# Chunk 3's normalized x through transposing transfers, eps as a column of x, PSUM banks by name, and a newly written order

## The chip, the cores and the metric

The kernel runs on one core of a Trainium2 chip. The metric is the device time of one execution in microseconds (us). The core has five engines with an instruction stream each: TensorE (PE, with its weight loads as PEld), VectorE (DVE), ScalarE (ACT), GpSimd (POOL) and SyncE (SP), which here issues transfers only. 16 DMA engines move the data.

## The reference

A linear-attention layer with a decay of its own for every channel, then a gated feed-forward block. B, H, S, D = 4, 8, 768, 48; the model width is H*D = 384, the feed-forward width 1536.

```python
for t in range(S):
    cur = einsum('bhd,bhe->bhde', u * k[t], v[t])
    y[t] = einsum('bhd,bhde->bhe', r[t], state + cur)
    state = w[t][..., None] * state + einsum('bhd,bhe->bhde', k[t], v[t])
x = y as (B*S, H*D)
rms = sqrt(mean(x * x) + 1e-06)
xn = x / rms * rms_g
g = xn @ w_gate
out = (g * sigmoid(g) * (xn @ w_val)) @ w_out
```

All inputs and the output are float32; the matmuls take bf16.

## The kernel before

The sequence is cut into chunks of 128 tokens, and a step is named `function.n.j`: n is the chunk (0 to 5), j mostly the batch (0 to 3) or, in the feed-forward part, a unit of work. Chunks 0 and 1 are the even and the odd tokens of the first 256, loaded together (384 KB per input and batch); later chunks are loaded one by one (192 KB).

Attention of one block (n, j): `ln` takes log w, `cs_mm`, `cs_k` and `cs_add` sum it over the tokens into PSUM, `exp_r` and `exp_k` exponentiate on ACT, `r_mul` (DVE) and `k_mul` (mostly POOL) multiply r and k into the tile `rk`. `rk` is transposed by PE (`rk_pe`, chunks 0 and 1) or by a transposing transfer (`rk_tr`, the others), `q_mm` makes the scores, `q_mask_e`, `q_copy_o` and `q_mask_o` mask them, `y_mm` makes y, `st_mm` and `st_new` carry the state. The bonus with u is `bonus_mul` (two products on POOL, tile `ruk`), `bonus_sum` (DVE, `diag`) and `bonus_v` (POOL, `ydiag`); `x_add` adds it to y.

Normalization of one block: `x_sq` sums the squares of 384 elements on ACT, `x_rstd` takes the reciprocal root (on ACT by Ln and Exp, or on POOL by a scaling and a power), `xn_mul` multiplies. For the feed-forward part, x must lie transposed in `xnt`. In chunks 0 to 3 `xn_pe` does this with three PE transposes into PSUM, and `xn_out` multiplies by rms_g on DVE on the way out. In chunks 4 and 5 `xn_tr` is a transposing transfer on SP's queue, and `xn_gain` multiplies by rms_g on POOL in place.

Feed-forward of one chunk: 12 units `gate_mm`, `silu` (ACT), `val_mm`, `h_mul` (DVE), then four `o_mm` (12 matmuls each, the last one of the last chunk in three pieces), `o_out`, `out_dma`. From chunk 1 on, a unit needs all four blocks of x of its chunk; in chunk 0 it needs two. The weights are cast on the way in by transfers that POOL issues: `load_gv.g.h` (gate h = 0, value h = 1; g = 1 is the larger part, feature blocks 4 to 11) and `load_wo`. All other transfers stand in SP's queue.

The order is a written list, `ORDER`: its 1096 steps are emitted one after the other, and each engine runs its own instructions in that order, waiting on semaphores for the others. Nothing is scheduled beyond that. `warm` steps are matmuls on zeros (13 at the start, 21 in between).

The eight PSUM banks form three rings: "a" has two banks, "b" two, "q" four. Each function names its ring, and `psum` takes the bank of that ring whose last use lies farthest back in the list. In the profile a bank reads as `ps_au`, `ps_bv`, `ps_qx` and so on. Sets such as `XN_DVE` or `CAST_ACT` say block by block on which engine a step runs.

Of the kernel before, what the change touches and what calls it, by code (L numbers as in the profile page):

```python
# [10 lines left out]
FP32 = mybir.dt.float32  # L11
# [16 lines left out]
warm.210.0 warm.211.0 warm.212.0 load_w.0.0 load_w.0.1 ln.0.0 ln.0.1 load_r.0.0 load_k.0.0 cs_k.0.0 exp_k.1.0  # L28
k_mul.1.0 cs_mm.0.0 exp_k.0.0 gu_mm.0.0 load_r.0.1 gu_out.0.0 load_k.0.1 exp_r.0.0 k_mul.0.0 bonus_mul.0.0 exp_r.1.0
cs_mm.0.1 cs_k.0.1 exp_r.0.1 load_w.0.2 exp_k.0.1 r_mul.0.0 r_mul.1.0 load_w.0.3 r_mul.0.1 bonus_mul.0.1 bonus_mul.1.0  # L30
exp_k.1.1 load_k.0.2 rk_pe.0.0 rk_tr.0.0 k_mul.1.1 rk_pe.1.0 warm.13.2 warm.14.2 warm.15.2 load_v.0.0 k_mul.0.1
rk_tr.1.0 bonus_sum.0.0 w_tot.0.0 load_gv.1.0 exp_r.1.1 load_r.0.2 q_mm.0.0 warm.16.0 q_mm.1.4 warm.17.1 warm.18.2
q_mask_e.0.0 r_mul.1.1 ln.0.2 ln.0.3 q_copy_o.0.0 cs_k.0.2 q_copy_o.1.4 exp_k.1.2 cs_mm.0.2 w_tot.0.1 q_mask_e.1.4
bonus_v.0.0 load_v.0.1 q_mask_o.1.4 exp_k.0.2 q_mm.1.0 rk_pe.1.1 warm.19.1 warm.20.1 warm.21.2 q_copy_o.1.0
bonus_sum.0.1 q_mask_e.1.0 exp_r.0.2 k_mul.1.2 cast_v.0.0 q_mm.0.4 warm.22.0 load_r.0.3 bonus_sum.1.0 load_k.0.3
exp_r.1.2 q_copy_o.0.4 cast_v.1.0 rk_pe.0.1 rk_tr.0.1 q_mask_o.1.0 cs_mm.0.3 q_mask_e.0.4 rk_tr.1.1 r_mul.1.2
bonus_v.1.0 exp_k.0.3 exp_r.0.3 y_mm.0.0 warm.23.0 q_mm.0.5 warm.24.0 warm.25.2 x_add.0.0 q_copy_o.0.5 y_mm.1.0
q_mask_o.0.5 cast_v.1.1 q_mask_e.0.5 cast_v.0.1 load_v.0.2 r_mul.0.2 x_sq.0.0 x_add.1.0 rk_pe.1.2 load_w.2.0
load_w.2.1 rk_tr.1.2 q_mm.0.1 warm.26.0 warm.27.0 warm.28.0 warm.29.2 q_copy_o.0.1 q_mask_e.0.1 exp_r.1.3 load_gv.1.1
q_mm.1.1 warm.30.2 x_rstd.0.0 st_mm.0.0 k_mul.0.2 w_tot.0.2 x_sq.1.0 q_mask_e.1.1 xn_mul.0.0 load_v.0.3 bonus_v.0.1  # L40
x_rstd.1.0 y_mm.0.1 rk_pe.0.2 q_copy_o.1.1 load_w.2.3 w_tot.0.3 xn_pe.0.0 st_new.0.0 xn_mul.1.0 x_add.0.1 cs_k.0.3
rk_tr.0.2 exp_k.1.3 xn_out.0.0 x_sq.0.1 bonus_mul.1.1 r_mul.0.3 xn_pe.1.0 warm.31.1 warm.32.2 xn_out.1.0 q_mm.1.5
warm.33.1 gate_mm.0.2 silu.0.2 gate_mm.0.3 silu.0.3 q_mask_o.1.1 q_mask_e.1.5 x_rstd.0.1 bonus_sum.1.1 q_copy_o.1.5
q_mm.1.2 r_mul.1.3 load_r.2.0 k_mul.1.3 bonus_v.1.1 bonus_mul.0.3 y_mm.1.1 xn_mul.0.1 x_add.1.1 gate_mm.0.5
gate_mm.0.4 q_mm.1.6 q_mask_e.1.2 load_gv.0.0 k_mul.0.3 q_copy_o.1.2 q_mask_e.1.6 silu.0.5 load_gv.0.1 bonus_mul.1.2
rk_pe.1.3 rk_tr.1.3 val_mm.0.3 xn_pe.0.1 xn_out.0.1 h_mul.0.3 q_copy_o.1.6 x_sq.1.1 val_mm.0.5 x_rstd.1.1 q_mm.1.7
xn_mul.1.1 rk_pe.0.3 bonus_mul.0.2 load_wo.0.0 val_mm.0.2 load_w.2.2 h_mul.0.5 q_copy_o.1.7 xn_pe.1.1 xn_out.1.1
st_mm.0.1 val_mm.0.4 load_r.2.1 gate_mm.0.10 h_mul.0.2 val_mm.0.10 ln.2.0 cast_v.1.2 ln.2.1 st_new.0.1 bonus_sum.1.2
q_mask_e.1.7 silu.0.4 q_mm.0.2 silu.0.10 rk_tr.0.3 load_v.2.1 gate_mm.0.9 gate_mm.0.8 q_copy_o.0.2 cast_v.0.2 silu.0.9
# [84 lines left out]
def kernel(  # L134
# [610 lines left out]
```

## Time and profile before

| | us |
|---|---|
| median of 3 runs | 200.35 (199.78, 203.26, 200.35) |
| span of the profiled execution, first to last instruction | 197.6 |
| PE busy in it | 191.5 (97%) |
| DVE, ACT, POOL busy | 156.4, 139.1, 127.5 |
| first feed-forward unit on PE starts | 25.79 |

Of the profiled execution the span is known, not its time by the runs' clock; the median of the runs lies 2.75 us above the span. "Busy" is the time in which an engine had at least one instruction in work. PE's matmuls overlap, each lasting some 0.16 us longer than its distance to the next, so a busy PE may still hold short gaps.

### The profile page before, as it was taken

The page shows a single profiled execution, that of the slowest core. Times are in us where ns is not written, and L with a number is a line of the kernel's source. Part 1 is how long each engine was busy: PE and PEld are TensorE (multiplying, and loading weights), DVE is VectorE, ACT ScalarE, POOL GpSimd, SP SyncE. Part 2 cuts the span into 40 slices and gives each one's busy share as a digit, 9 for nine tenths or more (in the row PEclk, how much of TensorE's full clock was granted, in tenths as well). Part 3 has the DMA queues.
Part 4 walks back from the last instruction along what each step waited for, and adds up shares of the span by engine and source line. Part 5 has one row for each costly group of instructions (what it writes and reads, how often), then busy time and mean ns, then how long its engine had stood idle before and what let it go on. Part 6 is the DMA issues. An engine that isn't in the chain of part 4 may idle for free.

```text
span 197.6 us, 4751 instructions
## 1 busy us (share of the span) xinstructions
PE 191.5 (97%) x1742; PEld 120.4 (61%) x1742; DVE 156.4 (79%) x315; ACT 139.1 (70%) x286; POOL 127.5 (64%) x181
## 2 busy tenths in 40 slices
PE   7899999999999999999999999999999999999994
PEld 3456677888665556655655655666655655555563
DVE  5699998999997999989799988997689842435530
ACT  3989998979997889795699875698556760514201
POOL 3399999988599759793969998599661544000000
PEclk9999999999999999999999999999999999999999
DMA  6999999999897999999999967924580021012112
GB/s 164 320 325 267 244 220 205 220 213 197 174 230 162 199 179 214 200 211 214 185 206 225 202 147 166 227 51 145 134 216 12 5 60 60 20 63 80 40 60 101
DMA packets 109807, 32.42 MB, mean 164 GB/s; under 512 B 104276, under 2 KB 108632, under 8 KB 109784
## 3 DMA queue, kind: packets, MB, share of 16 engines
q1 hardware_dynamic: 107744, 28.58, 63.4%
q0 software_dynamic: 2032, 3.54, 10.0%
q8 instruction: 13, 0.21, 0.5%
q14 instruction: 10, 0.08, 0.1%
q10 hardware_dynamic: 8, 0.00, 0.0%
HBM read 25.96 MB, written 4.72 MB: 155 GB/s over the span
## 4 chain that ended last, share of the span: by engine, by line
PE 83%; DMA 7%; POOL 6%; SPq 1%; issue 1%; ACT 0%; POOLq 0%
PE ps_bu L646 13%; PE ps_bv L646 12%; PE ps_av L646 11%; PE ps_au L646 11%; PE ps_qv L683 7%; PE ps_qx L683 6%; PE ps_qz L683 6%; DMA wv_sb<-in_moe_w_val_dram 5%; PE ps_qu L683 5%; DMA kt<-in_k_dram 2%; POOL ruk L464 1%; POOL ruk L465 1%; SPq L248 1%; POOL qts L536 1%; PE ps_qz L513 1%
## 5 line engine op out<-in xcount | busy, mean ns | idle before, releaser
L238 ACT ACTIVATE sg<-ps_av 128x512 bf16<-128x512 f32 x36 | 21.5, 596 | 27.1 <-PE ps_av L646 21.4
L683 PEld LDWEIGHTS <-ht 128*128 128x128 bf16 x312 | 28.6, 98 | 18.3 <-DVE ht L666 0.4
L646 PEld LDWEIGHTS <-wg_sb 128*128 128x128 bf16 x252 | 27.0, 114 | 16.6 <-issue 0.3
L646 PEld LDWEIGHTS <-wv_sb 128*128 128x128 bf16 x252 | 26.4, 114 | 16.0 <-DMA wv_sb<-in_moe_w_val_dram 0.7
L666 DVE TENSOR_TENSOR ht<-ps_bu,sg 128x512 bf16<-128x512 f32 x37 | 25.4, 687 | 10.7 <-PE ps_bu L646 8.3
L666 DVE TENSOR_TENSOR ht<-ps_bv,sg 128x512 bf16<-128x512 f32 x35 | 24.0, 686 | 9.9 <-PE ps_bv L646 8.5
L646 PE MATMUL ps_bu<-xnt,wv_sb 128*128 128x512 bf16 (+1 forms) x135 | 30.3, 343 | 0.5 <-DMA wv_sb<-in_moe_w_val_dram 0.5
L646 PE MATMUL ps_av<-xnt,wg_sb 128*128 128x512 bf16 (+1 forms) x126 | 29.4, 350 | 0.0
L646 PE MATMUL ps_au<-xnt,wg_sb 128*128 128x512 bf16 (+1 forms) x126 | 29.3, 349 | 0.1
L646 PE MATMUL ps_bv<-xnt,wv_sb 128*128 128x512 bf16 (+1 forms) x117 | 28.5, 358 | 0.0
L464 POOL TENSOR_TENSOR ruk<-rt,kt 128x384 f32<-128x384 f32 x24 | 24.0, 1002 | 1.9 <-DVE diag L469 1.4
L465 POOL TENSOR_TENSOR ruk<-ruk,u_bc 128x384 f32<-128x384 f32 x24 | 24.0, 1000 | 1.9
L238 ACT ACTIVATE sg<-ps_au 128x512 bf16<-128x512 f32 x36 | 21.5, 596 | 4.5 <-PE ps_au L646 3.3
L457 POOL TENSOR_TENSOR rk<-kt,ek 128x384 bf16<-128x384 f32 x20 | 19.8, 1001 | 6.6 <-DMA kt<-in_k_dram 5.5
L475 POOL TENSOR_TENSOR ydiag<-vt,diag 128x384 f32<-128x384 f32 x24 | 19.9, 836 | 1.0 <-DVE diag L469 1.0
L236 ACT ACT_TABLE_LOAD x14 | 18.0, 1283 | 1.9 <-PEq L729 1.6
L536 POOL TENSOR_SCALAR_AFFINE_SELECT qts<-qts 128x512 bf16<-128x512 bf16 x19 | 11.9, 637 | 11.2 <-ACT qts L533 8.0
L683 PE MATMUL ps_qv<-wo_sb,ht 128*128 128x384 bf16 (+1 forms) x96 | 15.5, 311 | 0.0
L581 ACT ACTIVATE junk<-xb 128x384 bf16<-128x384 f32 x24 | 12.5, 521 | 4.2 <-DVE xb L576 3.9
L469 DVE TENSOR_REDUCE diag<-ruk 128x8 f32<-128x384 f32 x24 | 13.0, 544 | 0.0
L683 PE MATMUL ps_qx<-wo_sb,ht 128*128 128x384 bf16 x72 | 12.7, 326 | 0.0
L683 PE MATMUL ps_qz<-wo_sb,ht 128*128 128x384 bf16 x72 | 12.7, 326 | 0.0
(212 smaller groups left out, 376.8 us busy)
## 6 DMA issues: line engine op xcount, KB each, us to landing
out_dram<-ob SPq DMA_DIRECT2D x19, 192.0 KB, 2.4
wt<-in_w_dram SPq DMA_DIRECT2D x16, 192.0 KB, 4.2
rt<-in_r_dram SPq DMA_DIRECT2D x16, 192.0 KB, 4.4
vt<-in_v_dram SPq DMA_DIRECT2D x16, 192.0 KB, 3.7
kt<-in_k_dram SPq DMA_DIRECT2D x16, 192.0 KB, 4.0
wt<-in_w_dram SPq DMA_DIRECT2D x4, 384.0 KB, 4.3
rt<-in_r_dram SPq DMA_DIRECT2D x4, 384.0 KB, 4.9
kt<-in_k_dram SPq DMA_DIRECT2D x4, 384.0 KB, 4.9
```

What stands on the lines that cost most here:

```text
L236: nc.scalar.preload_act_table_set(table_name)
L238: return nc.scalar.activation(**kw).ins
L457: eng.tensor_tensor(out=rk[:, n % 2, j, 1, :, 0:D], in0=inp["k", n, j], in1=bank["cs_k", n, j][:, 0:DM].rearrange("p (h d) -> p h d", h=H) ...
L464: eng.tensor_tensor(out=ruk[n, j], in0=inp["r", n, j], in1=inp["k", n, j], op=ALU.mult)
L465: eng.tensor_tensor(out=ruk[n, j], in0=ruk[n, j], in1=u_bc, op=ALU.mult)
L469: nc.vector.tensor_reduce(out=diag[n, j].rearrange("p h o -> p (h o)"), in_=ruk[n, j], axis=mybir.AxisListType.X, op=ALU.add)
L475: eng.tensor_tensor(out=ydiag[n, j], in0=inp["v", n, j], in1=diag[n, j].to_broadcast([128, H, D]), op=ALU.mult)
L536: nc.gpsimd.affine_select(out=qts[n, j][:, 1], in_=qts[n, j][:, 1], compare_op=ALU.is_ge if n < 2 and j // 4 < n else ALU.is_gt, fill=0.0, ...
L581: nc.scalar.activation(out=junk, in_=xb[n, j], func=AF.Square, accum_out=rstd[n, j][:, 0:1])
L646: nc.tensor.matmul(ps.rearrange("p (i t) -> p i t", t=cols.stop - cols.start)[:, i, :], lhsT=units(ws, c, fs.start + i), rhs=xnt[n][:, c, ...
L666: nc.vector.tensor_tensor(out=ht[n][:, fs, cols], in0=bank.pop(("v", n, f)).rearrange("p (i t) -> p i t", i=fs.stop - fs.start), in1=bank. ...
L683: nc.tensor.matmul(ps[:, cols], lhsT=ht[n][:, f, b * L:(b + 1) * L], rhs=wo_sb[:, f, cols], start=(f == 0), stop=(f == FC - 1))
```

## The change

Chunk 3 joins chunks 4 and 5: its four blocks are transposed by `xn_tr` and multiplied by `xn_gain` on POOL. x gets a 385th column that holds sqrt(eps * 384), so that the sum of squares, now scaled by 1/384 inside `x_sq`, includes eps; the reciprocal root on POOL is then one instruction, not two. Three lists name steps whose PSUM bank comes from another ring than their function's. The order is written anew in all its 1090 steps (17 fillers in between instead of 21), and so are the sets that choose engines: 15 value casts on ACT instead of 13, 11 products by the root on DVE instead of 6, two of the first transposes copied out on DVE instead of four, 17 separate masks on POOL instead of 19, seven roots on ACT instead of eight. ACT has 12 table loads instead of 14.

```diff
-warm.210.0 warm.211.0 warm.212.0 load_w.0.0 load_w.0.1 ln.0.0 ln.0.1 load_r.0.0 load_k.0.0 cs_k.0.0 exp_k.1.0
+warm.210.0 warm.211.0 warm.212.0 load_w.0.0 ln.0.0 cs_mm.0.0 exp_r.0.0 w_tot.0.0 exp_k.0.0 load_r.0.0 exp_r.1.0
...
+    MOVED_Q = "cs_k.2.3 cs_k.3.1 ..."
+    MOVED_A = "cs_k.2.1 cs_k.3.0 ..."
+    MOVED_B = "cs_k.1.1 cs_r.0.0 ..."
...
+    moved = {}
+    for c, names in (("q", MOVED_Q), ("a", MOVED_A), ("b", MOVED_B)):
+        for x in names.split():
+            name, n, j = x.split(".")
+            moved[name, int(n), int(j)] = c
 
     def psum(ring, key, shape, dtype=FP32):
+        ring = moved.get(key, ring)
         slots = rings[ring]
...
+    xrow = const.tile([128, NXB, DM + 16], FP32)
+    nc.vector.memset(xrow[:, :, DM:DM + 1], (eps * DM) ** 0.5)
...
     def x_add(n, j):
-        xb[n, j] = pt.tile([128, DM], FP32, name="xb", bufs=NXB)
-        nc.vector.tensor_tensor(out=xb[n, j], in0=bank.pop(("y", n, j)),
+        k = min((x for x in range(NXB) if xslots[x][0] < at[0]), key=lambda x: xslots[x])
+        xslots[k] = [xlast[n, j], NXB + at[0]]
+        xb[n, j] = xrow[:, k, 0:DM + 1]
+        nc.vector.tensor_tensor(out=xb[n, j][:, 0:DM], in0=bank.pop(("y", n, j)),
...
     def x_sq(n, j):
-        nc.scalar.activation(out=junk, in_=xb[n, j], func=AF.Square, accum_out=rstd[n, j][:, 0:1])
+        nc.scalar.activation(out=junk[:, 0:DM + 1], in_=xb[n, j], func=AF.Square, scale=DM ** -0.5,
+                             accum_out=rstd[n, j][:, 0:1])
...
     def x_rstd(n, j):
-            act(LN_EXP, out=ss, in_=ss, func=AF.Ln, scale=1.0 / DM, bias=eps_col)
+            act(LN_EXP, out=ss, in_=ss, func=AF.Ln)
...
-            nc.gpsimd.tensor_scalar(out=ss, in0=ss, scalar1=1.0 / DM, scalar2=eps, op0=ALU.mult, op1=ALU.add)
             nc.gpsimd.tensor_tensor(out=rstd[n, j][:, 1:2], in0=ss, in1=mhalf, op=ALU.pow)
```

SP's queue at the very start, where the loads of the first 256 tokens stand (`wt`, `rt`, `kt` are w, r, k of a batch; the first of each is batch 0). Before:

```order
L248 DMA wt_167<-in_w_dram 128x8x96
L248 DMA wt_169<-in_w_dram 128x8x96
L248 DMA rt_174<-in_r_dram 128x8x96
L248 DMA kt_176<-in_k_dram 128x8x96
L248 DMA rt_203<-in_r_dram 128x8x96
L248 DMA kt_207<-in_k_dram 128x8x96
```

Now:

```order
L257 DMA wt_167<-in_w_dram 128x8x96
L257 DMA rt_190<-in_r_dram 128x8x96
L257 DMA kt_194<-in_k_dram 128x8x96
L257 DMA wt_208<-in_w_dram 128x8x96
L257 DMA wt_252<-in_w_dram 128x8x96
L257 DMA vt_294<-in_v_dram 128x8x96
```

r and k of batch 0 have moved ahead of w of batch 1, and k of batch 1 behind v of batch 0.

POOL's queue up to the larger part of the value weights (`wv_sb4`). Five rows are the same in both orders and stand ahead of these: one `k_mul` and two `bonus_mul`, of two rows each. Before:

```order
L464 TENSOR_TENSOR ruk_245<-rt_174,kt_176 128x384
L465 TENSOR_TENSOR ruk_245<-ruk_245,u_bc_76 128x384
L457 TENSOR_TENSOR rk_131<-kt_207,ek_235 128x8x48
L350 DMA wg_sb4_138<-in_moe_w_gate_dram 128x3x1024
L475 TENSOR_TENSOR ydiag_346<-vt_278,diag_283 128x384
L536 AFFINE_SELECT qts_314<-qts_314 128x512
L536 AFFINE_SELECT qts_363<-qts_363 128x512
L475 TENSOR_TENSOR ydiag_440<-vt_278,diag_402 128x384
L536 AFFINE_SELECT qts_474<-qts_474 128x512
L384 CAST vb_500<-vt_348 128x384
L350 DMA wv_sb4_140<-in_moe_w_val_dram 128x3x1024
```

Now:

```order
L471 TENSOR_TENSOR rk_129<-kt_315,ek_270 128x8x48
L550 AFFINE_SELECT qts_266<-qts_266 128x512
L489 TENSOR_TENSOR ydiag_406<-vt_294,diag_311 128x384
L478 TENSOR_TENSOR ruk_414<-rt_317,kt_315 128x384
L479 TENSOR_TENSOR ruk_414<-ruk_414,u_bc_76 128x384
L357 DMA wg_sb4_136<-in_moe_w_gate_dram 128x3x1024
L550 AFFINE_SELECT qts_289<-qts_289 128x512
L489 TENSOR_TENSOR ydiag_479<-vt_294,diag_275 128x384
L471 TENSOR_TENSOR rk_129<-kt_482,ek_376 128x8x48
L478 TENSOR_TENSOR ruk_524<-rt_317,kt_315 128x384
L479 TENSOR_TENSOR ruk_524<-ruk_524,u_bc_76 128x384
L357 DMA wv_sb4_138<-in_moe_w_val_dram 128x3x1024
```

The value weights now have one bonus pair (`ruk`, two rows) and one `k_mul` (`rk`) more ahead of them, and one mask and one cast fewer.

SP's queue where chunk 3 is normalized, now (before, no transposing transfer of `xn` stood there); the two transfers of batches 0 and 3 stand just ahead, `rt_2012` is r of chunk 4, batch 0:

```order
L622 DMA_TRANSPOSE xnt_2157<-xn_2211 128x3x128
L719 DMA out_0_dram<-ob_1938 128x384
L267 DMA rt_2012<-in_r_dram 128x8x48
L267 DMA vt_2221<-in_v_dram 128x8x48
L719 DMA out_0_dram<-ob_1845 128x384
L622 DMA_TRANSPOSE xnt_2157<-xn_2246 128x3x128
```

And POOL's queue there, now; the first row is the root of batch 2, `ruk_2298` the bonus of chunk 4, batch 0:

```order
L606 TENSOR_TENSOR rstd_2162<-rstd_2162,mhalf_126 128x1
L640 TENSOR_TENSOR xnt_2157<-xnt_2157,gT_77 128x3x128
L478 TENSOR_TENSOR ruk_2265<-rt_1553,kt_1926 128x384
L479 TENSOR_TENSOR ruk_2265<-ruk_2265,u_bc_76 128x384
L640 TENSOR_TENSOR xnt_2157<-xnt_2157,gT_77 128x3x128 x2
L478 TENSOR_TENSOR ruk_2298<-rt_2012,kt_1661 128x384
L479 TENSOR_TENSOR ruk_2298<-ruk_2298,u_bc_76 128x384
L640 TENSOR_TENSOR xnt_2157<-xnt_2157,gT_77 128x3x128
```

The four multiplications by rms_g stood on DVE before, and the last of them now follows the bonus of the next chunk.

More of the change, by code (lines that the diff above doesn't have):

```diff
@@ L325 @@
     nc.vector.memset(mhalf, -0.5)
-    eps_col = small.tile([128, 1], FP32)
-    nc.vector.memset(eps_col, eps)
     lw = persist.tile([128, 2, SB, H, PD], BF16)
@@ L360 @@
     bank = {}
+    xrow = const.tile([128, NXB, DM + 16], FP32)
+    nc.vector.memset(xrow[:, :, DM:DM + 1], (eps * DM) ** 0.5)
+    xlast = {(int(b), int(c)): i for i, (a, b, c) in enumerate(x.split(".") for x in ORDER.split())
+             if a in ("x_sq", "xn_mul")}
+    xslots = [[-2, i] for i in range(NXB)]
     def pair(t, q):
@@ L382, in cast_v @@
             nc.scalar.copy(out=vb[n, j], in_=inp["v", n, j])
+        elif (n, j) in CAST_DVE:
+            nc.vector.tensor_copy(out=vb[n, j], in_=inp["v", n, j])
         else:
```

233 lines of the change are left out of this document (116 added, 117 removed).

## The prediction

> **What bounds the kernel now.** I read the page from the top: the engines' shares and the granted clock, then the busy time in four stretches, then what TensorE (PE) waited for, then its instructions in order of time at the places that the change touches.
>
> ```profile
> span 197.6 us, 4751 instructions
> PE 191.5 (97%) x1742; PEld 120.4 (61%) x1742; DVE 156.4 (79%) x315; ACT 139.1 (70%) x286; POOL 127.5 (64%) x181
> PEclk9999999999999999999999999999999999999999
> ...
> 0.00:25.80 25.80, 23.15 (x269) 13.87 (x270) 21.95 (x61) 21.13 (x43) 19.09 (x33) 1.00 1.05 265
> 25.80:45.00 19.20, 18.71 (x254) 16.42 (x255) 18.21 (x33) 17.05 (x33) 17.73 (x25) 1.00 1.12 210
> 45.00:160.00 115.00, 114.98 (x1012) 70.03 (x1011) 103.18 (x202) 90.95 (x194) 86.96 (x120) 1.00 0.79 167
> 160.00:197.60 37.60, 34.70 (x212) 20.12 (x209) 13.09 (x22) 10.02 (x19) 3.67 (x6) 1.00 0.19 61
> ```
>
> The last four rows are stretches: length, then busy us and instructions of PE, PE's weight loads, DVE, ACT and POOL, the clock, the DMA share. From 45 to 160 us PE is busy for 114.98 of 115 us, and after that until its end: there PE is the bound, and only PE work that goes away, or a new wait of PE, moves the time. The other engines have slack there, though DVE little (103 of 115 us). The front is different. Busy PE flatters it: the matmuls overlap, and part of them are fillers on zeros.
>
> ```profile
> 4.22 0.53 PE L377 MATMUL ps_qx<-zero 128*128 128x384 bf16 x1
> 4.54 0.53 PE L377 MATMUL ps_qz<-zero 128*128 128x384 bf16 x1
> ...
> 21.59 0.32 PE L377 MATMUL ps_qz<-zero 128*128 128x384 bf16 x1
> 21.75 0.32 PE L377 MATMUL ps_bu<-zero 128*128 128x384 bf16 x1
> ...
> 25.79 0.82 PE L646 MATMUL ps_au<-xnt,wg_sb 128*128 128x256 bf16 x6
> 26.44 0.82 PE L646 MATMUL ps_av<-xnt,wg_sb 128*128 128x256 bf16 x6
> ```
>
> Columns are start, duration, instruction. The start-to-start distance is what a matmul takes from PE: a filler 0.32 us at first and 0.16 us later, a unit of six feed-forward matmuls 0.65 us (26.44 - 25.79). The first unit starts at 25.79 us. The front is fed by DVE, POOL and the weights' transfers:
>
> ```profile
> 8.13 0.56 DVE L457 TENSOR_TENSOR rk<-kt,ps_qv 128x384 bf16<-128x384 f32 x1 [1.67 <-DMA kt<-in_k_dram]
> ...
> 25.09 0.55 DVE L619 TENSOR_TENSOR xnt<-ps_qx,gT 128x384 bf16<-128x384 bf16 x1
> ...
> 1.92 1.26 SPq L248
> 3.23 4.80 DMA kt<-in_k_dram
> 20.98 9.76 DMA wv_sb<-in_moe_w_val_dram
> ...
> 30.79 0.84 PE L646 MATMUL ps_bu<-xnt,wv_sb 128*128 128x256 bf16 x6 [0.49 <-DMA wv_sb<-in_moe_w_val_dram]
> ```
>
> DVE starts its first product when k lands (3.23 + 4.80 = 8.03 us) and works without a gap to the second block of normalized x at 25.64. POOL issues the larger value-weight transfer at 20.98; it takes 9.76 us, and PE waits 0.49 us for it. That is one of only four waits of PE in the whole list, the first and the last of which are
>
> ```profile
> PE ps_qu L377 <- DVE half_of L303: 1.0, 1, 1.0
> ...
> PE ps_qv L377 <- DVE rkT L489: 0.3, 1, 0.3
> ```
>
> **The change part by part.**
>
> *Transposes of chunk 3.* Twelve PE transposes (four blocks of three) and four DVE multiplications go.
>
> ```profile
> 104.85 0.33 PE L612 MATMUL ps_qz<-ident,xn 128*128 128x128 bf16 x3
> 105.02 0.33 PE L612 MATMUL ps_qx<-ident,xn 128*128 128x128 bf16 x3
> 105.19 0.33 PE L410 MATMUL ps_au<-lw,mask_lt 128*128 128x384 bf16 x1
> ...
> xnt<-xn SPq DMA_TRANSPOSE x8, 2.3
> rt<-in_r_dram SPq DMA_DIRECT2D x16, 192.0 KB, 4.4
> ...
> 136.45 1.95 PE ps_qz L683 x12
> ```
>
> Three transposes take 0.17 us from PE (105.02 - 104.85), four blocks **0.7 us**, all in the stretch where PE is the bound: it comes off whole. The DVE multiplications are 4 x 0.55 = 2.2 us and hidden. What takes their place: four transposing transfers on SP's queue, 2.3 us each to land, and four multiplications on POOL. Chunks 4 and 5 go that way already, and no wait of PE is listed there. What is queued behind them matters more. On SP the transfer of batch 1 has r of chunk 4, batch 0, two places behind it; on POOL the bonus of that r stands ahead of the last multiplication of chunk 3, for which the first gate unit of chunk 3 waits. The chain from the reciprocal root of batch 1: its product with x (0.55 as the DVE row above), a transposing transfer (2.3 at most, since only its issue holds up the next), r (4.4 to landing), the bonus (2.0), the multiplication (0.84), together 10.1 us. PE has in the meantime three units of 0.65, three output products of 1.95 each and 0.7 us of small matmuls, 8.5 us. So a stall of up to 1.6 us is possible; but the root may run ahead of PE, whose own work on that stretch is not tied to it. Below nothing is excluded here: no PE work goes beyond the transposes. I take 0, nearest to chunks 4 and 5, and keep +1.6.
>
> *The front.* SP now loads w, r, k of batch 0 first, before w of batch 1; k is third instead of fourth, so up to 1.3 us sooner (one issue, 1.26 us). DVE has 38 instructions from its first product to the second block of normalized x in both orders; the new one has one wide instruction in place of one of the smallest, at most 0.6 us more. So the first gate unit would come between 0.7 us sooner and, if DVE is left waiting early on (its first sum over the bonus still needs three POOL products), 0.6 us later. But the value weights bind first. POOL's rows:
>
> ```profile
> L464 POOL TENSOR_TENSOR ruk<-rt,kt 128x384 f32<-128x384 f32 x24 | 24.0, 1002 | 1.9 <-DVE diag L469 1.4 <-DMA kt<-in_k_dram 0.5
> L465 POOL TENSOR_TENSOR ruk<-ruk,u_bc 128x384 f32<-128x384 f32 x24 | 24.0, 1000 | 1.9
> L475 POOL TENSOR_TENSOR ydiag<-vt,diag 128x384 f32<-128x384 f32 x24 | 19.9, 836 | 1.0 <-DVE diag L469 1.0
> L457 POOL TENSOR_TENSOR rk<-kt,ek 128x384 bf16<-128x384 f32 x20 | 19.8, 1001 | 6.6 <-DMA kt<-in_k_dram 5.5 <-ACT ek L238 1.0
> L536 POOL TENSOR_SCALAR_AFFINE_SELECT qts<-qts 128x512 bf16<-128x512 bf16 x19 | 11.9, 637 | 11.2 <-ACT qts L533 8.0 <-DMA vt<-in_v_dram 3.2
> L590 POOL TENSOR_TENSOR rstd<-rstd,mhalf 128x1 f32<-128x1 f32 x16 | 8.9, 556 | 1.3
> L625 POOL TENSOR_TENSOR xnt<-xnt,gT 128x384 bf16<-128x384 bf16 x8 | 6.6, 844 | 4.3 <-DMA xnt<-xn 3.4 <-PE ps_bu L646 1.0
> L589 POOL TENSOR_SCALAR rstd<-rstd 128x1 f32<-128x1 f32 x16 | 3.0, 189 | 8.9 <-ACT junk L581 8.2
> ...
> wv_sb<-in_moe_w_val_dram POOLq DMA_DIRECT2D x1, 384.0 KB, 7.5
> ...
> 42.16 0.85 PE L646 MATMUL ps_bu<-xnt,wv_sb 128*128 128x256 bf16 x6
> ```
>
> Ahead of the larger value-weight transfer POOL took 20.98 - 8.03 = 12.95 us after k. The new order puts one bonus pair (2.0) and one k product (1.0) more ahead of it and one select and one cast (0.64 each, the cast taken at the select's row) fewer: +1.7, so 14.7 us. With k at 6.8 to 8.0 us it is issued at 21.5 to 22.7 and lands 9.76 us later, at 31.3 to 32.4, which is 0.5 to 1.7 us after the 30.74 of now. Against that, PE has more done by then: one more group of eight transposes and two more score products of eight, at 0.057 us for a transpose (0.17 / 3) 0.45 us and 0.45 to 0.9 us, in all 0.9 to 1.35 us. The balance lies between 0.5 - 1.35 = -0.85 and 1.7 - 0.9 = +0.8; below that, up to the 1.3 us of k may come on top if DVE and not the weights bind. I take the early k, since the transfer order says it outright, and the smaller work: 0.5 - 0.9 = **-0.4 us**. The four fillers fewer (0.16 us each) are worth nothing by themselves: where a filler stood, PE waited for DVE.
>
> *Roots, casts, copies, eps, banks.* POOL loses the 0.19 us of scaling in each of its roots, two selects and two casts, and gains four multiplications (3.4 us); ACT loses two of 14 table loads; single casts and copies move between ACT, POOL and DVE. All of it lies under a full PE after 45 us and costs nothing there. The cover is thinnest on DVE: it gains five products of at most 0.55 us and loses 2.2 us, so about +0.5 us on 103 of 115; without cover, that 0.5 us would be the price. Drawing PSUM banks from any ring takes nothing from an engine. It can only remove waits of PE, of which the long stretch shows none.
>
> *The end.*
>
> ```profile
> 194.03 0.67 PE L683 MATMUL ps_qu<-wo_sb,ht 128*128 128x96 bf16 x12
> ...
> 194.74 0.24 ACT L692 COPY ob<-ps_qu 128x96 f32<-128x96 f32 x1 [0.54 <-PE ps_qu L683]
> ...
> L236 ACT ACT_TABLE_LOAD x14 | 18.0, 1283 | 1.9 <-PEq L729 1.6
> ```
>
> The last output piece is now 192 columns wide, not 96. PE's sum is unchanged; the copy after it grows from 0.24 us, at most to double: +0.1 us taken.
>
> *Sum*: span 197.6 - 0.7 - 0.4 + 0.1 = 196.6 us. The profiled execution's time is known as its span only; the median of the three runs, 200.35, stands 2.75 us above it, and I add this: **199.3 us**.
>
> One rule speaks against the change. In the rows above the fillers go from 0.32 to 0.16 us apart after about 4 us of matmuls, and the granted clock stays at 9 or more in every slice. The Trainium skill, "TensorE: Matmul & The Clock Gate", Part 1, says that the array runs at half clock until it has been busy for a window of about 3.4 us, and falls back after an idle window as long. The trace agrees with its first half (a halving of the distance between 4.54 and 21.59 us); no row shows a fall back. By the rule, fewer fillers could cost clock; it enters as the fourth case below.
>
> **The rivals.**
>
> *The front gains more (197.6 us).* If the first unit follows DVE and the weights are not waited for, the early k gives 1.2 us and the work done ahead 0.9 us: 197.6 - 0.7 - 2.1 + 0.1 = 194.9, and 2.75. For it: DVE is gapless from 8.13 us on. Against it: POOL's longer queue ahead of the weights.
>
> *Weights late (201.7 us), slower than before.* POOL sets the front. Between the two value-weight issues the new order has one k product less, but three selects, one cast and two roots more, against one root with its scaling (-1.0 + 1.9 + 0.64 + 1.1 - 0.75): +1.9 us on the 10.8 us of now, so the second is issued at 34.2 us or later and lands 7.5 us after that, 41.7. PE uses it at 42.16 now. With k at 8.0 us it lands at 42.9, and each wait of POOL for a diagonal or a mask adds. Then both weights cost: +0.8 and some 1.2, so 197.6 - 0.7 + 2.0 + 0.1 = 199.0, and 2.75. It decides at a landing of the first weights after about 32.2 us, or of the second after 42. Against it: the second transfer would follow the first at a greater distance and may land sooner than in 7.5 us.
>
> *Nothing comes of it (200.4 us).* The transposes' 0.7 us come back as a wait of the first gate unit of chunk 3, the chain of 10.1 against 8.5 us above.
>
> *The clock falls back (201 us).* If PE idled long enough in the first 25 us, one stretch of 3.4 us would run with matmuls twice as far apart, as at 4.22 us: up to 1.7 us more, 199.3 + 1.7. The granted clock of before speaks against it.
>
> **How the numbers follow.** Forecast 50% (198.4 to 200.2), front gains more 22%, weights late 18%, nothing 7%, clock 3%. The front's case spreads down to 195.5, the late weights' up to 203. The range takes 196.0 to 202.0 us: it leaves a third of the front's case and a third of the late weights' out, some 14%. Two per cent, about what a measurement can tell from no change here, are 196.3 and 204.4 us: faster 8%, within 89%, slower 3%.
>
> **What would show it.** Right: no transposes on PE between chunk 2's last and chunk 4's units, four transposing transfers and four multiplications for chunk 3, the first gate unit at 25 to 26.5 us, the larger value weights landing between 31 and 32.5 us, and PE at 115 of 115 us from 45 us on. Wrong: a wait of PE at the first gate unit of chunk 3 for POOL; a wait for the value weights above 1.5 us; distances of 0.32 us after 10 us; or a first gate unit before 24 us, which would mean that the front was bound by the order and not by DVE's sum.

## The result and the profile after

The changed kernel takes 208.1 us in the median of four runs (206.43 to 209.85), the kernel before 200.06; the ratio is **1.039 (1.033 to 1.045)**: slower. The forecast was 199.3 us. Runs that took over 1.5% longer than the fastest of their kernel stay out of every ratio, but not out of the medians.

The page of the changed kernel, top to bottom: its span, the busy time of each engine, the busy share of the DMA engines in 40 slices, and the chain that ended last, by engine and by line.

```profile
span 205.5 us, 4679 instructions
PE 191.3 (93%) x1711; PEld 120.5 (59%) x1726; DVE 158.0 (77%) x315; ACT 136.1 (66%) x280; POOL 126.2 (61%) x166
DMA  6999999999998899999977998602494012220012
PE 48%; DMA 13%; DVE 12%; POOL 10%; ACT 6%; issue 5%; SPq 4%; ACTq 0%; POOLq 0%; DVEq 0%
```

PE's sum is nearly the old one, 191.3 us against 191.5, in a span 7.9 us longer: the time is PE waiting. PE now holds 48% of the chain (83% in the kernel before), and transfers, DVE and POOL 35%. The stretches show where (length, then busy us of PE, its weight loads, DVE, ACT, POOL, the clock, the DMA share, GB/s):

```profile
30.00:45.00 15.00, 13.95 (x179) 12.83 (x177) 13.09 (x23) 12.31 (x22) 13.66 (x19) 1.00 1.13 210
45.00:60.00 15.00, 14.37 (x158) 10.81 (x158) 14.74 (x33) 14.31 (x34) 10.33 (x13) 1.00 1.02 201
60.00:75.00 15.00, 13.96 (x121) 7.80 (x121) 12.78 (x24) 9.23 (x18) 12.06 (x16) 1.00 0.91 190
75.00:90.00 15.00, 13.61 (x128) 8.50 (x131) 14.18 (x32) 13.39 (x34) 12.45 (x15) 1.00 1.01 206
90.00:105.00 15.00, 14.05 (x127) 8.23 (x129) 11.96 (x22) 8.88 (x20) 6.79 (x10) 1.00 1.05 219
105.00:120.00 15.00, 12.55 (x83) 7.19 (x84) 12.50 (x26) 10.50 (x20) 12.33 (x16) 1.00 0.83 164
120.00:165.00 45.00, 44.73 (x366) 26.26 (x370) 34.47 (x63) 27.88 (x61) 30.34 (x39) 1.00 0.54 117
```

PE is idle for 75 - 68.54 = 6.5 us between 45 and 120 us, where it had been full, and for 0.3 us after that to 165. The waits of PE in the list are many and short: nine between 45 and 120 us, 5.8 us in all. But for the 1.1 us of a filler at the very start, its longest are

```profile
PE ps_bu L424 <- DVE ht L678: 1.6, 1, 1.6
PE ps_au L628 <- DVE xn L611: 1.5, 2, 1.2
PE ps_av L424 <- DVE st L566: 0.9, 1, 0.9
PE ps_av L515 <- ACT sg L247: 0.7, 1, 0.7
PE ps_av L658 <- POOL xnt L640: 0.5, 1, 0.5
```

The fourth, and 0.3 us of the second, lie before 45 us. The last is the wait that the prediction looked for, of chunk 3's first gate unit for POOL: 0.5 us. Three of the other four name an instruction that has nothing to do with the data of the waiting matmul, but is the last reader of its PSUM bank (feed-forward product, state and activation): in the first, `cs_mm` (L424) of chunk 4 waits at 106.45 us for DVE's feed-forward product, which reads `ps_bu` until then. Why DVE was late there, the chain in order of time tells:

```profile
97.36 4.79 DMA rt<-in_r_dram
...
102.22 1.01 POOL ruk L478
...
103.30 1.00 POOL ruk L479
...
104.31 0.45 POOL vb L398
104.75 1.03 POOL rstd L606 x2
...
105.81 0.70 DVE xn L611
...
106.88 0.54 DVE diag L483
107.41 1.21 DVE ht L678 x2
```

An r of chunk 4, issued at 97.36 us, lands at 102.15. POOL's bonus product waits for it, and behind it in POOL's queue stand the cast and two reciprocal roots of chunk 3; behind the roots' product stand DVE's feed-forward products; behind them PE. A late input of one chunk stops the feed-forward of another through three engines that work in written order.

### The profile page after: what moved, and what is told of

It reads as the page before. It is cut to its first block, busy times and chain, and to the rows that moved or that the text cites. A ratio compares the mean times of both kernels' runs of the same rounds, so it can differ in the third digit from the quotient of the medians.

```text
span 205.5 us, 4679 instructions
## 1 busy us (share of the span) xinstructions
PE 191.3 (93%) x1711; PEld 120.5 (59%) x1726; DVE 158.0 (77%) x315; ACT 136.1 (66%) x280; POOL 126.2 (61%) x166
## 4 chain that ended last, share of the span: by engine, by line
PE 48%; DMA 13%; DVE 12%; POOL 10%; ACT 6%; issue 5%; SPq 4%; ACTq 0%; POOLq 0%; DVEq 0%
DMA wt<-in_w_dram 6%; PE ps_bv L658 4%; DMA kt<-in_k_dram 4%; PE ps_av L658 3%; SPq L267 3%; PE ps_bu L658 3%; PE ps_au L658 3%; PE ps_qu L658 3%; PE ps_qv L658 3%; PE ps_bv L695 3%; PE ps_au L695 3%; PE ps_qz L658 3%; POOL rk L471 2%; POOL ruk L478 2%; DMA rt<-in_r_dram 2%
## 5 line engine op out<-in xcount | busy, mean ns | idle before, releaser
L247 ACT ACTIVATE sg<-ps_av 128x512 bf16<-128x512 f32 x16 | 9.6, 599 | 15.0 <-PE ps_av L658 7.7
L597 ACT ACTIVATE junk<-xrow 128x385 bf16<-128x385 f32 x24 | 12.6, 527 | 4.4 <-DVE xrow L592 4.2
L640 POOL TENSOR_TENSOR xnt<-xnt,gT 128x384 bf16<-128x384 bf16 x12 | 10.0, 844 | 8.1 <-PE ps_qz L658 4.8
L606 POOL TENSOR_TENSOR rstd<-rstd,mhalf 128x1 f32<-128x1 f32 x17 | 9.3, 552 | 9.2 <-ACT junk L597 9.2
L247 ACT ACTIVATE lw<-wt 128x384 bf16<-128x384 f32 (+1 forms) x20 | 11.4, 585 | 4.1 <-DMA wt<-in_w_dram 4.1
L658 PE MATMUL ps_av<-xnt,wg_sb 128*128 128x512 bf16 (+1 forms) x55 | 12.9, 344 | 0.7 <-POOL xnt L640 0.5
L658 PE MATMUL ps_bv<-xnt,wg_sb 128*128 128x512 bf16 (+1 forms) x41 | 10.6, 365 | 0.1
L695 PE MATMUL ps_bv<-wo_sb,ht 128*128 128x384 bf16 x60 | 10.6, 326 | 0.0
L695 PE MATMUL ps_au<-wo_sb,ht 128*128 128x384 bf16 x60 | 10.6, 326 | 0.0
L247 ACT ACTIVATE sg<-ps_bv 128x512 bf16<-128x512 f32 x13 | 7.8, 601 | 3.8 <-PE ps_bv L658 2.8
```

The source lines that it names most:

```text
L247: return nc.scalar.activation(**kw).ins
L597: nc.scalar.activation(out=junk[:, 0:DM + 1], in_=xb[n, j], func=AF.Square, scale=DM ** -0.5, accum_out=rstd[n, j][:, 0:1])
L658: nc.tensor.matmul(ps.rearrange("p (i t) -> p i t", t=cols.stop - cols.start)[:, i, :], lhsT=units(ws, c, fs.start + i), rhs=xnt[n][:, c, ...
L695: nc.tensor.matmul(ps[:, cols], lhsT=ht[n][:, f, b * L:(b + 1) * L], rhs=wo_sb[:, f, cols], start=(f == 0), stop=(f == FC - 1))
```

## The experiments

All ratios are to the kernel before on the same chip. "Old order" is the order of the kernel before, "cheap transfers" are input transfers of chunks 2 to 5 in runs of 1536 bytes, from other addresses, so that these kernels compute other numbers. Where an expectation counts feed-forward work in us, it took a unit at 1.28 us, twice its 0.65: its 11.5 us are 5.85 us, its 7 us are 3 to 4 us. Where moved steps found no free PSUM bank in their ring (a_x3pe, a_x3pe2, b_x3_cover, a_delay and both b_adv, as in a_ring), the tile takes one of another ring, so these runs can change banks as well.

**1. Chunk 3 by transposing transfers, alone (b_x3).**

```diff
-    GAIN_POOL = (4, 5)
+    GAIN_POOL = (3, 4, 5)
-xn_pe.3.1 xn_out.3.1 ... xn_pe.3.3 xn_out.3.3
+xn_tr.3.1 xn_gain.3.1 ... xn_tr.3.3 xn_gain.3.3
```

> The kernel before, with one part of the change alone: normalized x of chunk 3 by four transposing transfers and four POOL multiplications, written where its PE transposes and DVE multiplications stood. Theory one (the new order lets the inputs of chunks 2 to 4 arrive late; the transposing transfers are not the cause): within 1 us of the kernel before, 199.4 to 201 us. Rival (the four transposing transfers and the POOL multiplications cost the 7 us, since they stand in the stretch where the transfer engines are busy all the time): 204 us or more, with PE waiting at chunk 3's gate units.

207.8 us, ratio 1.038 (1.031 to 1.045): the rival's result, and as much as the whole change. Its stretch, its wait, and PE's and the other rows at that place:

```profile
105.00:120.00 15.00, 8.81 (x56) 4.64 (x55) 6.03 (x15) 7.64 (x16) 10.85 (x14) 0.86 0.74 165
PE ps_bu L647 <- POOL xnt L626: 6.0, 1, 6.0
...
108.26 0.62 ACT L598 ACTIVATE xn<-xb,rstd 128x384 bf16<-128x384 f32 x1
...
108.14 1.97 SPq L259 DMA_DIRECT2D rt<-in_r_dram  x2
110.21 3.93 SPq L607 DMA_TRANSPOSE xnt<-xn  x2
...
116.05 0.83 POOL L626 TENSOR_TENSOR xnt<-xnt,gT 128x384 bf16<-128x384 bf16 x1
...
108.82 2.11 PE L684 MATMUL ps_qx<-wo_sb,ht 128*128 128x384 bf16 x12
116.93 1.44 PE L647 MATMUL ps_bu<-xnt,wv_sb 128*128 128x512 bf16 x3 [6.00 <-POOL xnt L626]
...
122.58 0.81 PE L647 MATMUL ps_av<-xnt,wg_sb 128*128 128x512 bf16 x3
```

PE has nothing left at 110.9 us. The last product of x ends at 108.9, its transfer stands behind two loads of r until 110.21, POOL puts a k product of chunk 4 (1.0 us) ahead of the last multiplication, and that ends at 116.88: 8.0 us from product to matmul, 6.0 of them uncovered. Then the clock falls: the units from 116.93 on take 1.22 to 1.27 us of PE instead of 0.65 until 122.58 (116.93 to 118.16 for the first). The Trainium skill, "TensorE: Matmul & The Clock Gate", Part 1, has the array go back to half clock after an idle window of about 3.4 us; the trace agrees, with a wait of 6.0 us, a granted clock of 0.86 in the stretch and units nearly twice as long behind it. But so long a wait isn't needed here: in a_edf (experiment 4) two units take 1.27 us each from 90.64 to 93.19, at a granted clock of 0.50 from 90 to 93 us, behind waits of 1.75 and 0.58 us with only small matmuls (48 rows) between them. That is a different picture from the changed kernel's, which has the same transfers and a clock of 1.00.

**2. The changed kernel without them (a_x3pe, a_x3pe2).**

```diff
-xn_tr.3.0 ... xn_gain.3.0
+... xn_pe.3.0 xn_out.3.0        # a_x3pe: where xn_gain stood
+xn_pe.3.0 xn_out.3.0 ...        # a_x3pe2: where xn_tr stood
```

> The changed kernel with chunk 3 back on PE: each transposing transfer and its multiplication become three PE transposes and a DVE multiplication, both written where the multiplication stood. Theory one (late inputs): 206 to 209 us, as the changed kernel, with PE still idle between 45 and 105 us. Rival (transposing transfers): most of the loss comes back, 200 to 203 us.

> The changed kernel with chunk 3 back on PE, cleanly: three PE transposes and the DVE multiplication of each block are written where its transposing transfer stood (the earlier try wrote them just ahead of the first unit, and held x up). If the transposing transfers are what costs in the changed kernel, 200 to 203 us, with PE's idle time at 105 to 120 us gone. If the changed order costs by itself (attention of chunk 3 begun earlier than its inputs come), the idle time between 45 and 105 us stays at 3 us or more and the time at 204 to 208 us.

213.3 us, ratio 1.064 (1.056 to 1.072), for the first, which is not clean, since its PE transposes wait for x right ahead of the units. In the second they stand where the transfers stood: 209.1 and 210.6 us against 199.7 for the kernel before, two runs only (the other two took 212.8 and 213.5), too few for an interval.

```profile
60.00:75.00 15.00, 13.07 (x119) 7.25 (x117) 12.70 (x23) 8.37 (x16) 11.97 (x16) 1.00 0.95 199
75.00:90.00 15.00, 13.83 (x137) 8.73 (x134) 14.28 (x33) 13.37 (x35) 12.19 (x14) 1.00 1.04 211
90.00:105.00 15.00, 12.34 (x117) 6.95 (x115) 11.97 (x23) 8.62 (x20) 7.49 (x11) 1.00 1.03 215
```

Without a single transposing transfer for chunk 3, PE is idle for 5.8 us between 60 and 105 us. So the changed order loses without the transfers, and the transfers' own cost and the order's do not add up. How much the order alone costs the run doesn't tell: it was written for the transfers, and here PE transposes, DVE multiplications and some other banks are put into it.

**3. Cheap transfers (a_dense, b_dense).**

```diff
-        nc.sync.dma_start(out=inp[which, n, j], in_=t[j, :, n * L:(n + 1) * L, :].rearrange("h t d -> t h d"))
+        nc.sync.dma_start(out=inp[which, n, j].rearrange("p h d -> p (h d)"),
+                          in_=t.rearrange("b h s d -> (b h s d)")[...].rearrange("(p x) -> p x", p=L))
```

> The changed kernel with the same number of bytes in each input transfer of chunks 2 to 5, but read as one run of 1536 bytes a partition instead of eight of 192 bytes (from other addresses, so the inputs of those chunks are other numbers). Theory one (late inputs, since the transfer engines are full from 5 to 105 us): PE's waits between 45 and 120 us go, and the time falls to 200 us or less. Rival (PSUM banks drawn from any ring, or the engine sets, tie PE to ACT and DVE): no more than 2 us of the 7.5 us come back, 205 to 208 us.

> The kernel before with its input transfers of chunks 2 to 5 read as one run of 1536 bytes a partition instead of eight of 192 (the inputs of those chunks are other numbers). It is the control for the same edit of the changed kernel (200.3 us). If PE bounds the kernel before from 45 us on, cheaper transfers give nothing: 198.5 to 200.5 us. If its transfers bound it as well, 197 us or less, and the changed kernel with cheap transfers would still be losing 3 us to something else.

The changed kernel 200.3 us, ratio 1.002 (0.999 to 1.005): all of the loss is gone. The control 202.3 us, 1.011 (1.004 to 1.018): it gained nothing. Three of its four runs took 202.1 to 202.7 us and one 199.7, as the kernel before. In the profiled one (202.1) the loss lies between 30 and 45 us, where PE was busy for 12.96 us against 14.51 before: PE waits 1.6 us for DVE's k product of chunk 1, and DVE 2.65 us for that k, waits that the kernel before doesn't have.

```profile
PE ps_qu L501 <- DVE rk L457: 1.6, 1, 1.6
```

So cheap transfers have a cost of their own in the old order, and what they do there (experiment 7) is read against this control. Rows of the changed kernel with cheap transfers:

```profile
30.00:45.00 15.00, 14.14 (x181) 12.92 (x180) 14.55 (x25) 13.54 (x27) 13.76 (x19) 1.00 1.12 294
45.00:60.00 15.00, 15.00 (x162) 11.08 (x161) 14.13 (x32) 14.40 (x34) 11.43 (x14) 1.00 0.63 151
60.00:75.00 15.00, 15.00 (x141) 8.69 (x140) 14.57 (x27) 10.72 (x21) 13.45 (x17) 1.00 0.85 257
```

PE is full again from 45 to 75 us, and idle for 0.6 us in the next 30; of the nine waits two are left, 0.3 and 0.2 us. In the stretch from 30 to 45 us the same DMA share moves 294 GB/s instead of 210. The Trainium skill, "DMA: Bandwidth & Descriptors", Specifications, asks for 512 bytes or more for the full rate; this comparison agrees. It shows that the loss hangs on the input transfers: on when the inputs land, or on how long they hold the queue and the transfer engines against the transposing transfers. It doesn't show which input. It also shows that the banks' names, which are the same here, cost no more than 0.5 us between 45 and 120 us by themselves.

**4. Sequence and queue of the loads (a_edf, a_vact).**

```diff
# a_edf: 63 places of the list differ, each load's place goes to the load needed first
# a_vact:
-        nc.sync.dma_start(out=inp[which, n, j], ...)
+        (nc.scalar if which == "v" else nc.sync).dma_start(out=inp[which, n, j], ...)
```

> The changed kernel with the loads of chunks 2 to 5 in other places of the order: the places are kept, but each gets the load that is needed first among those whose buffer is free; 63 of the written steps differ, all of them loads. Theory one (the sequence of the loads is what costs): half of the loss or more comes back, 200 to 204 us. Rival (the loads are late because of what stands between them, or are not the cause): 206 to 209 us.

> The changed kernel with the sixteen loads of v of chunks 2 to 5 issued by ACT's queue instead of SP's; their written places stay. Theory D (SP's queue in order is what makes the inputs late): the idle time of PE between 45 and 120 us, 6.4 us, falls by half or more, 201 to 205 us. Rival (the transfer engines themselves are full): no gain, 206 us or more.

207.5 us, 1.036 (1.028 to 1.045), and 209.8 us, 1.049 (1.040 to 1.059). Neither brought anything back. In the first the waits between 45 and 120 us are others, 3.8 of 5.1 us of idle time behind transposing transfers of `rk`: this sequence is no cure, which isn't to say that none is. The second can't decide between the queue and the transfer engines, since ACT, which now issues, became a wait of its own:

```profile
PE ps_av L515 <- ACT sg L247: 2.6, 1, 2.6
PE ps_qx L658 <- ACT sg L247: 1.4, 1, 1.4
```

**5. PSUM banks (a_ring).** All three lists of names are empty.

```diff
-    MOVED_Q = "cs_k.2.3 cs_k.3.1 ..."
+    MOVED_Q = ""
+        if not any(x[0] < at[0] for x in rings[ring]):
+            ring = next(c for c in "qab" if any(x[0] < at[0] for x in rings[c]))
```

> The changed kernel with no bank named: each PSUM tile comes from its kind's ring as before, and from another only where that ring has none free. Theory C: no change, 206.5 to 209 us. Rival (banks shared between gate, value and attention tiles make PE wait for ACT and DVE): 204 us or less.

233.7 us, 1.170 (1.166 to 1.174): neither theory. With banks by kind PE is busy for only 23.0 of the first 30 us, and its longest wait is a value unit's for the last reader of its bank:

```profile
PE ps_bv L660 <- DVE ht L680: 3.0, 5, 0.9
```

This order needs its named banks; that some of them cost in the changed kernel when inputs are late, as the wait of L424 suggests, is not excluded (with cheap transfers they don't, experiment 3).

**6. The root (b_root).** The old order with the column of eps and one POOL instruction for the root.

```diff
-            nc.gpsimd.tensor_scalar(out=ss, in0=ss, scalar1=1.0 / DM, scalar2=eps, op0=ALU.mult, op1=ALU.add)
             nc.gpsimd.tensor_tensor(out=rstd[n, j][:, 1:2], in0=ss, in1=mhalf, op=ALU.pow)
```

> The kernel before with eps in a column of x, and so a reciprocal root of one POOL instruction instead of two, alone. All theories: no change, 199 to 201 us, since POOL's 0.19 us an instruction lie under a full PE.

199.4 us, 0.9994 (0.9977 to 1.0010): nothing, as expected.

**7. Is it the chain or the queue that costs in the old order (b_x3_dense, b_x3_cover, b_x3_fast, b_x3_fast_dense).**

```diff
# b_x3_cover
-o_mm.2.1 exp_r.4.2 exp_k.4.2 w_tot.4.2 val_mm.3.5
+o_mm.2.1 exp_r.4.2 exp_k.4.2 w_tot.4.2 ... o_mm.2.3 ... o_mm.2.2 ... val_mm.3.5
# b_x3_fast
-x_rstd.3.3 exp_r.4.1 h_mul.2.3 ... xn_mul.3.3 ... load_r.4.2 load_r.5.1 ... xn_tr.3.3 xn_gain.3.3
+x_rstd.3.3 exp_r.4.1 h_mul.2.3 xn_mul.3.3 xn_tr.3.3 ... load_r.4.2 load_r.5.1 ... xn_gain.3.3 k_mul.4.0
-    XN_DVE = sel("02 21 23 42 43 51")
+    XN_DVE = sel("02 21 23 32 33 42 43 51")
```

> The kernel before with chunk 3 alone by transposing transfers (207.8 us), and its input transfers of chunks 2 to 5 read in runs of 1536 bytes as above (other numbers). Theory A (the longer chain of chunk 3 is late because the input transfers around it fill the queue and the transfer engines): the wait of 6 us at chunk 3's first unit goes, 199 to 201 us. Theory B (the chain, product on ACT, transposing transfer, multiplication on POOL, is by itself longer than PE's other work): the wait stays above 3 us, 203 us or more.

206.6 us, 1.037 (1.033 to 1.041), with a wait of 4.1 us left: theory B, the chain is too long whatever the inputs' transfers. Against the control (1.011) it is 2.6%.

> The kernel before with chunk 3 alone by transposing transfers (207.8 us), and two output products of chunk 2 (1.95 us each on PE) moved from behind chunk 3's units to in front of them, with their copies and transfers. If the loss is a wait of PE for the last block of chunk 3's x and the clock that falls back behind it, 3.9 us more of cover take 3.9 us off a wait of 6 us, and the clock does not fall back: 201 to 204 us, with a wait of 2 us left. If instead the transposing transfers slow down the whole stretch, 206 us or more.

205.4 us, 1.027 (1.021 to 1.032). The wait fell to 1.9 us and the clock stayed at 1.00, as expected, but not the time: PE was busy for only 13.17 of 15 us from 135 to 150, where the two output products had stood and the next one now waits 1.7 us for DVE's feed-forward product.

> The kernel before with chunk 3 by transposing transfers (207.8 us), and its chain shortened: the products of blocks 2 and 3 on DVE right behind their roots instead of on ACT behind the table load and exponentials of chunk 4, each transposing transfer right behind its product on the queue and so ahead of two loads of r, the k product of chunk 4 behind the last multiplication on POOL. In the trace of the transposing transfers alone the last product is written at 108.9 us, its transfer issued at 110.2, lands at 114.3, and PE starts at 116.9. If that chain is the whole loss, the last product comes at 106 to 107 us and PE's wait falls below 2.5 us without the clock falling back: 199 to 202.5 us. If the transposing transfers hold up others, 205 us or more.

204.5 us, 1.022 (1.018 to 1.027). The chain is cured: the last multiplication ends at 112.27 us, and PE goes on at 112.31. Then it stops for another reason:

```profile
110.66 1.61 POOL L626 TENSOR_TENSOR xnt<-xnt,gT 128x384 bf16<-128x384 bf16 x2
...
112.31 0.81 PE L647 MATMUL ps_bu<-xnt,wv_sb 128*128 128x512 bf16 x3 [0.52 <-ACT lw L239]
...
111.22 2.68 SPq L259 DMA_DIRECT2D rt<-in_r_dram  x2
...
115.51 0.55 DVE L452 TENSOR_TENSOR rk<-rt,ps_au 128x384 bf16<-128x384 f32 x1 [3.64 <-DMA rt<-in_r_dram]
...
116.12 1.18 PE L647 MATMUL ps_au<-xnt,wg_sb 128*128 128x512 bf16 x3 [2.01 <-DVE rk L452]
```

SP issues r of chunk 4 at 111.22 us, behind all four transposing transfers, which wait for their x and hold the queue for 1.2 us each; shortening the chain put the last two of them ahead of that r. In the kernel before it was

```profile
106.12 2.16 SPq L258 DMA_DIRECT2D rt<-in_r_dram  x2
```

> The kernel before with chunk 3 by transposing transfers and the shortened chain (204.5 us), and the input transfers of chunks 2 to 5 in runs of 1536 bytes (other numbers). With the old chain the cheap transfers brought back 1.3 us of 8. If the loss has two conditions, a chain that is too long and an r of chunk 4 that the transfers bring too late, both are removed here: 198.5 to 201 us. If something else is left, 203 us or more.

203.4 us, 1.022 (1.016 to 1.028). Against the kernel before the ratio is the same, against the control half of the loss stays. The profiled execution is the slowest of the four (205.95 us, the others 203.05 to 203.43), so its times can't be set beside those above; in it PE is idle for 3.2 us from 105 to 120, against 3.6 with the old transfers, and SP, which now issues the loads sooner, stands still for 7.0 us from 98.1 on until the x of a transposing transfer is there. That r is issued at 113.9 us: cheap transfers don't help what stands behind a waiting transfer in the queue.

**8. The transfers without their chain (b_dummy), and another queue (b_x3_act).**

```diff
# b_dummy: the old order, PE transposes kept, and ahead of each block's
+        nc.sync.dma_start_transpose(x, bank["xn", n, j])     # x is read by nothing
# b_x3_act: b_x3_fast with
+        (nc.scalar if n == 3 else nc.sync).dma_start_transpose(xnt[n][:, :, j * L:(j + 1) * L], ...)
```

> The kernel before, chunk 3 by PE transposes as it was, with four transposing transfers of the same x added in front of them, into a buffer that nothing reads. Nobody waits for them, but they stand in SP's queue ahead of the loads of chunk 4. Theory D (SP issues in order and has no time to spare until 115 us, so that a transposing transfer pushes the input loads behind it): r of chunk 4 lands later and PE waits for DVE's r product, 201 to 206 us. Rival (only the longer chain of x costs): 199 to 200.5 us.

202.8 us, 1.013 (1.006 to 1.020). Four transfers that nobody waits for cost 3.0 us, 1.5 of them by theory D's path:

```profile
108.90 1.96 SPq L260 DMA_DIRECT2D rt<-in_r_dram  x2
...
114.10 0.55 DVE L453 TENSOR_TENSOR rk<-rt,ps_au 128x384 bf16<-128x384 f32 x1 [2.47 <-DMA rt<-in_r_dram]
...
114.71 0.84 PE L652 MATMUL ps_au<-xnt,wg_sb 128*128 128x512 bf16 x3 [1.47 <-DVE rk L453]
```

Another 1.1 us are waits of PE, near 120 us, for transposing transfers of `rk` (0.50 and 0.61), which SP issues from 116.48 us on instead of 109.97. The run doesn't part the place in the queue from the load on the transfer engines.

> The kernel before with chunk 3 by transposing transfers and the shortened chain (204.5 us, where PE waited 2.0 us for DVE's product with an r that SP had issued at 111.2 us behind the transposing transfers), with these four transfers issued by ACT's queue instead of SP's. Theory D: the loads go back to their old times and PE no longer waits for r: 199 to 201.5 us, if ACT's own 1.2 us for each issue stays hidden. Rival (the transfer engines are full, and it does not matter which queue issues): 203.5 us or more.

206.4 us, 1.031 (1.023 to 1.039). SP issues the two loads of r from 106.97 us on, nearly as in the kernel before, as theory D said; for the time it is inconclusive: the issues of 1.2 us each stand in ACT's own order, and PE waits 4.2 us for ACT's next activation. The step from SP's queue to another's was not tried on an idle engine.

**9. Attention of chunk 3 earlier, or later (b_adv, a_delay, b_adv_dense).**

```diff
# b_adv, for one step of many; a_delay does the reverse in the changed order
-val_mm.2.1 gate_mm.2.5 ... gate_mm.2.9 rk_tr.3.3 val_mm.2.10      # behind 57 units
+val_mm.2.1 rk_tr.3.3 q_copy_o.3.1 gate_mm.2.5                     # behind 52
```

> The kernel before, chunk 3 by PE transposes as it was, with one thing taken from the changed order: the attention steps of chunk 3 (loads, logarithm, sums, exponentials, products, transposes, scores, x) are written up to 7 us of feed-forward work earlier, tapering to nothing at both ends; PSUM banks by the first free ring where the own one is full. In the changed kernel the last transposed r and k of chunk 3 stand 11.5 us of feed-forward work earlier than before. Theory C (the changed order starts the attention of chunk 3 earlier, its inputs cannot come earlier because the transfer engines are full, and PE starves between 60 and 105 us): PE idle for 2 us or more there, 202 to 206 us. Rival (the early attention is free; only the transposing transfers cost): 199 to 201 us.

> The kernel before with the attention of chunk 3 written up to 7 us of feed-forward work earlier (216.2 us), and the input transfers of chunks 2 to 5 read in runs of 1536 bytes a partition (other numbers). In the trace without the cheap transfers the last r of chunk 3 was issued at 72.5 us, as before, and landed at 76.6; DVE waited for it with a feed-forward product queued behind, and PE starved. Theory C: with cheap transfers most of the 16 us come back, 200 to 206 us. Rival (the moved steps collide in the engines' queues or in PSUM banks, whatever the transfers): 211 us or more.

216.2 us, 1.080 (1.075 to 1.086), and with cheap transfers 216.1 us, 1.082 (1.075 to 1.088). The loss is there, as theory C said, but far too large, and cheap transfers leave it: theory C falls for this kernel. The chain, here with cheap transfers, suggests another reason: four table loads of 1.28 us stand in it within 8 us (74.41, 76.79, 79.10 and 81.01), because logarithms of chunk 3 came to stand between activations of the feed-forward (b_adv has 18 table loads, the kernel before 14). That they make up the loss was not tested.

So b_adv is no copy of the changed order, which has 12 table loads, and tells little on it.

> The changed kernel with the attention steps of chunk 3, without its loads, written up to 7 us of feed-forward work later, tapering at both ends; the transposing transfers stay. Theory C: PE's idle time between 60 and 105 us (4 us in the changed kernel) falls to 1.5 us or less, but the last block of chunk 3's x comes late for its first units, so that a wait for POOL's multiplication of 2 to 6 us appears there, as with the transposing transfers alone: 203 to 208 us. Rival (loads or banks, not the place of the attention): the idle time at 60 to 105 us stays at 3.5 us or more.

230.4 us, 1.153 (1.145 to 1.160). The wait for POOL's multiplication appears (2.9 us), but the idle time at 60 to 105 us grows to 13.9 us; a logarithm of chunk 5 also overwrites one of chunk 3 that is still to be read, so some numbers differ. Shifting one chunk by a rule breaks more than it tests. No run beat the kernel before.

## Why the prediction was wrong

*The bound.* The reading was right for the trace that it was read from: PE full from 45 us on. The failed step is the sentence "All of it lies under a full PE after 45 us and costs nothing there", with the new order of 1090 steps under it. The full PE was a property of the old order, not of the stretch. For the root the step holds (experiment 6). For the order it doesn't: in the changed kernel 6.5 us of idle time came up under it, all but 0.6 us of which are gone with cheap transfers (experiment 3), and without any transposing transfer of chunk 3 the order still loses (experiment 2). The warning stood in the quoted rows: a DMA share of 1.05 and 1.12 up to 45 us and 0.79 on the average up to 160. The input transfers had no slack to give to this order, and no term of the sum asked for them.

*Banks.* "It can only remove waits of PE" was wrong in its form: a bank's last reader is a wait, too. The longest wait of PE after 45 us in the changed kernel is one for a bank, and how much hangs on the banks' names in this order is seen in experiment 5.

*Transposes of chunk 3.* The twelve transposes are gone from PE, and the wait in the changed kernel is the 0.5 us of POOL, within the 0 to 1.6 us allowed. But that it fits is luck, because the wait came by another path than the working's (transfer, r and bonus):

```profile
113.95 3.95 DMA xnt<-xn
...
117.97 0.84 POOL xnt L640
```

POOL's bonus of that r was done 1.0 us before the last multiplication. That one waits for the last transposing transfer, which takes 3.95 us to land, not 2.3: its root is there at 108.83 us, but its product stands in DVE's order until 112.48, and the transfer in SP's until 113.95. With the old order the chain is short of cover by 6.0 us and costs 8.2 with the clock. What the working left out was ACT's queue (the product of the last block waited for a table load and exponentials of chunk 4), the loads of r ahead on SP, and that r itself would then be late. The last is the cost that remains when the chain is cured, and it was looked for on the wrong side: I counted what stands behind the transposing transfer as a delay of the transfer's own consumers, not of the loads' consumers.

*The front.* The first gate unit came at 26.37 us (25 to 26.5 forecast), the larger value weights were issued at 21.89 (21.5 to 22.7), and PE waited 0.32 us for them:

```profile
26.37 0.83 PE L658 MATMUL ps_au<-xnt,wg_sb 128*128 128x256 bf16 x6
...
21.89 0.81 POOL L357 DMA_DIRECT2D wv_sb<-in_moe_w_val_dram  x1
...
31.67 0.84 PE L658 MATMUL ps_qv<-xnt,wv_sb 128*128 128x256 bf16 x6 [0.32 <-DMA wv_sb<-in_moe_w_val_dram]
```

The gain of 0.4 us did not come: PE was busy for 40.86 us up to 45 us, 1.0 less than before, of which the four fillers explain 0.64. The misses of the front are small against the stretch behind it.

*The term of 2.75 us.* It compared a span with the median of other executions. In every run with both numbers on record the time lies 1.7 to 1.8 us above the span (207.22 and 205.5 for the changed kernel), so the same sum gives about 198.3 us, and the forecast stood 1 us nearer to the result by this mistake alone. The rival of 200.4 us drops the front's 0.4 us as well: with only the transposes' 0.7 us coming back the sum gives 200.0.

*The rivals.* All that ended above the forecast by more than 2 us lay in the front; none lay between 45 and 165 us, where more than 80% of the loss is (6.7 of 7.9 us). The clock that falls back was named in the right terms, and came, in experiments 1 and 4, at places that were not thought of; in the changed kernel it stayed at 1.00.

*What is settled and what is open.* Shown: the transposing transfers alone cost 8 us in the old order, first by their chain (6.0 us of waiting, and the clock), and, with the chain cured, also by the loads behind them in SP's queue (4.8 us are left, 2.0 of them PE's wait for the product with the late r; transfers that nothing reads cost 3.0). Shown: the changed order avoids that one wait and loses as much in many small ones; a loss is there without the transfers too, and it is gone with cheap inputs. Argued from one place of the chain only: that a late input passes through POOL's, DVE's and PE's orders. Open: which of the moved steps make the inputs too late, and whether queue or transfer engines hold them up; the one other sequence of the loads that was tried didn't cure it.

## What to carry to other kernels

That an engine is full tells what the present order hides, not what another order will. Before a rewritten order is costed at nothing, read the DMA share and the input loads in the same stretch, and follow each queue that works in written order past the moved step: what stands behind it is late by all that it waits for. A transfer that replaces PE work must be priced by its place among the loads, and a dummy of it that nothing reads measures what it costs without its chain.

## What was not expected of the hardware

A transposing transfer that nothing reads was not free: four cost 3.0 us. Input transfers with runs of 1536 instead of 192 bytes moved 294 instead of 210 GB/s at the same DMA share, and yet the kernel before did not gain from them (1.011, 1.004 to 1.018). A wait of 6.0 us nearly halved PE's rate for the next 5.65 us, 116.93 to 122.58, and waits of 1.75 and 0.58 us close together did it too (a_edf, 90.64 to 93.19).
